# Residual products placed ahead of step 2's, and step 1's pieces as six products of 256 columns instead of three of 512

## The chip, the cores and the metric

The kernel runs on one core of one Trainium2 chip. The metric is device microseconds of one execution, the median of the runs shown; lower is better. Before the change it is 996.77 us (three runs, 996.63 to 997.63).

## The reference

The input x is 8 batches of 3136 rows of 256 numbers in float32. What is computed is the real part of a two-dimensional Fourier transform, and a normalised two-layer network on it:

```python
X = np.fft.fft(x, axis=1)
X = np.fft.fft(X, axis=2)
x = X.real.astype(np.float32)
mu = np.mean(x, axis=-1, keepdims=True)
var = np.mean((x - mu) ** 2, axis=-1, keepdims=True)
xn = (x - mu) / np.sqrt(var + 1e-06) * g_ln
ch = np.maximum(xn @ w_ch1, 0.0) @ w_ch2
return (x + ch).astype(np.float32)
```

w_ch1 is 256 x 1024 and w_ch2 is 1024 x 256.

## The kernel before

**The work.** The transform along the 3136 rows is done in two steps of smaller products. The symmetry of a real transform is used, so that only 1567 rows and two single ones for each batch pass through the rest; the second half comes out of sums and differences at the end. The transform along the 256 columns is folded into the network's first weights, and is done once more for the sum at the end, the *residual*.

- *Step 1* (`step1`, lines 251 to 269): seven pieces for each batch. The input is folded on GpSimd (`fold_zw`, `fold_eo`) and split into a high part (`fold_hi`, ScalarE) and a low part (`fold_lo`, GpSimd), both float32r. Each piece is multiplied by the table t1 in three passes (`PASSES`, line 341: high table with low piece, low table with high piece, high with high), each one product of 512 columns (line 266). All three add up in one bank of PSUM. ScalarE copies it out (line 269), and it goes to device memory and comes back in another order (`store1`, `relayout`). Batch 0 is done in another way ahead of the main loop (lines 259 and 261).
- *Step 2* (`step2`, lines 303 to 339): 64 units, eight for each batch. A unit is four float32 products of 98 or 99 columns (line 313); the first unit of a batch has another of 50 columns (line 317). The profile shows each float32 product as two instructions, so eight records for a unit. The result is a stretch of rows of the transform, and is cut into *chunks* of 256: ScalarE writes the high part (line 334) and a full copy (line 336), VectorE the low part (line 338). A unit can end in two chunks.
- *Network, first layer* (`moe1_a`, line 358): six float32r products of 256 columns for one chunk and one of eight groups of hidden units; ScalarE and VectorE make sum and difference of their two halves (lines 363 to 365). `moe1_b` (lines 372 and 373) applies the maximum with zero and splits the result into high and low parts.
- *Network, second layer* (`moe2`, line 408): twelve float32r products of 256 columns, added up in two banks (tags `acc0` and `acc1`, for even and odd chunks) over the eight groups.
- *Residual* (`residual`, lines 430 to 440): for each chunk two halves (c, 0) and (c, 1), each two float32 products of 129 and 130 columns (line 438), eight records in the profile. `residual_e` (ScalarE) and `residual_y` (VectorE) take it out of PSUM and make mean and variance; `finish` (lines 483 to 490, VectorE) adds the network's result, and `store_out` writes it.

**The order.** All engines but SyncE run in an order that is written out by hand (`tc.manual_schedule`). The main loop (lines 836 to 843) goes through *slots*, eight for each chunk, s = 8c + f:

```python
moe1_b(s - 1)
moe1_a(s)
for fn, args in late.get(s, ()):
    fn(*args)
moe2(s - lag)
for fn, args in after.get(s, ()):
    fn(*args)
```

A slot thus has six products of line 358 and twelve of line 408, all float32r and 256 columns wide, and whatever `late` and `after` hold for it. Everything else is placed in these two lists by lines 616 to 684:

- Step 2's units stand in `after` of slot 8c + 5, for those whose first row falls into chunk c + 1 (lines 626 to 636). Most of these slots have one unit, fourteen have two. The second unit of a slot uses the bank of PSUM with tag `y`, the first that with tag `fft`. The low part (line 338) is made in `late` of the next slot.
- The residual of chunk c stands in `after` of the same slot 8c + 5 (line 666), added after step 2's units. The only exception is chunk 37, where it is inserted ahead of them (lines 670 and 671). I call such a slot, and the eight up to the next of its kind, *block* c. A block with two units is a *double* block. Blocks 0 and 1 have the residual in slots of their own.
- The residual's two banks are those of `acc` that the chunk before has used: (c, 0) needs line 489 of half 0 of chunk c - 1 to be done, (c, 1) that of half 1, which stands in `late` of slot 8c + 4.
- In batches 2 to 7 five of the seven pieces of step 1 stand in the slot behind such a group: one slot later in a block with one unit, two slots later in a double block (`behind`, lines 637 to 639). The other two are at `need - 46` and `need - 45 - b % 2` (line 645), so that in batches 3, 5 and 7 two pieces share a slot. Step 1 uses the bank with tag `y`; of two pieces in one slot the second uses `fft` (`joined`, lines 247 to 249).
- A piece's loads, folds and casts are placed at fixed distances ahead of its slot, its store behind it (lines 653 to 663).

**Shapes.** The residual's first product has 129 columns, its second 130. A table (`shape`, lines 426 to 428) gives, for 12 blocks (7, 13, 19, 25, 31, 40 and 42 to 47), another width (130) to the first product or another order of the two, for one half or both.

Of the kernel before, what the change touches and what calls it, by code (L numbers as in the profile page):

```python
# [20 lines left out]
F32 = mybir.dt.float32  # L21
# [13 lines left out]
LC = NCH - 1  # L35
# [111 lines left out]
def tile_kernel(ctx: ExitStack, tc: tile.TileContext, x, g_ln, w1, w2, tu, tab, tz, ty, tw, out):  # L147
    nc = tc.nc
# [4 lines left out]
    psum = ctx.enter_context(tc.tile_pool(name="psum", bufs=1, space=bass.MemoryType.PSUM))  # L153
# [8 lines left out]
    t1_hi = weights.tile([128, 128], F32R, name="t1_hi")  # L162
    t1_lo = weights.tile([128, 128], F32R, name="t1_lo")
# [6 lines left out]
    ty_s = const.tile([128, 2, 130], F32, name="ty_s")  # L170
# [57 lines left out]
    def alloc1(b):  # L228
        if b not in s1:
            s1[b] = work.tile([128, NS, 2, 128], F32, tag="s1", name=f"s1_{b}", bufs=1)  # L230
            scratch[b] = dram.tile([NS, 128, D], F32, tag="scratch", name=f"scratch{b}")
# [12 lines left out]
        if p1 == NS:  # L244
            nc.scalar.copy(zmu[:, b % 2, 127:128], ps[:KP, 2, 0:1])

    def joined(b, i):

        return i > 0 and steps1[b][i] == steps1[b][i - 1]

    def step1(b, i):
        alloc1(b)
        ps = psum.tile([128, 2, 2, 128], F32, name=f"ps1_{b}_{i}", bufs=1 if b else 2,
                       tag=("fft" if joined(b, i) else "y") if b else f"acc{i % 2}")
        if b == 0:
            z, w = zw.pop((b, i))
            for h in range(2):
                o = ps[:, :, h]
                nc.tensor.matmul(o, tu_s[:, 0:128], z, start=(h == 0), stop=False,  # L259
                                 skip_group_check=True)  # L260
                nc.tensor.matmul(o, tu_s[:, 128 * h:128 * h + 128], w, start=False, stop=True,  # L261
                                 skip_group_check=True)
        else:
            p = pieces.pop((b, i))
            for n, (ti, xi) in enumerate(PASSES):
                nc.tensor.matmul(ps, (t1_hi, t1_lo)[ti], p[xi],  # L266
                                 start=(n == 0), stop=(n == 2))
        s = s1[b][:, 2 * i:2 * i + 2]
        nc.scalar.copy(s[:, :, :, :127], ps[:, :, :, :127])  # L269

# [18 lines left out]
    def first_token(m):  # L289
        b, j = divmod(m, 8)  # L290
        return b * REG + max(gb[2 * j] - 2, 0)
# [102 lines left out]
    acc = {}  # L394
# [21 lines left out]
    def mixed():  # L416
# [6 lines left out]
                                op0=ALU.mult)  # L423
        mixes.append(t)

    shape = {(7, 0): (130, 0), (13, 1): (130, 0), (19, 0): (130, 0), (19, 1): (130, 0),
             (25, 0): (129, 1), (25, 1): (129, 1), (31, 1): (129, 1),
             **{(c, 0): (130, 0) for c in (40, 42, 43, 44, 45, 46, 47)}}

    def residual(c, i):  # L430
        ps = psum.tile([128, 2, 130], F32, tag="y" if i > 1 else f"acc{(c + 1) % 2}",
                       name=f"psy{c}_{i}", bufs=1 if i > 1 else 2)
        t0 = 120 if i == 3 else 128 * i
        ck = mixes.pop() if i == 2 else chunk[c][0][:, :, t0:t0 + 128]
        n0, j0 = shape.get((c, i), (129, 0))
        for j in (j0, 1 - j0):
            n = (n0, 130)[j]
            nc.tensor.matmul(ps[:, j, :n], ck[:, j], ty_s[:, j, :n], start=(j == j0), stop=True,  # L438
                             skip_group_check=True)
        res[c, i] = ps  # L440

    def residual_e(c, i):
# [160 lines left out]
    def finish_w2(n):  # L603
        _, e, f = conv.pop(f"w2_{n}")
        nc.vector.scalar_tensor_tensor(out=f, in0=f, scalar=2.0 ** -20, in1=e, op0=ALU.mult,
                                       op1=ALU.mult)
        return f
# [8 lines left out]
    after, late = {}, {}  # L616

    def add(s, fn, *args):

        after.setdefault(s, []).append((fn, args))  # L620

    def add_late(s, fn, *args):

        late.setdefault(s, []).append((fn, args))

    first = {}
    for m in range(3, 64):
        s = 8 * (first_token(m) // CW) - 3
# [8 lines left out]
    def behind(s):  # L637

        return s + 1 + (len(first[s]) > 1)

    steps1 = {1: [17, 20, 23, 26, 28, 30, 33]}
    casts = dict(zip(steps1[1], (12, 15, 20, 22, 23, 27, 28)))
    for b in range(2, NB):
        need = 8 * (b * REG // CW) - 3
        steps1[b] = sorted([need - 46, need - 45 - b % 2] +
                           [behind(need - d) for d in (56, 40, 32, 24, 16)])
    for b in range(1, NB):
        need = 8 * (b * REG // CW) - 3
        at = steps1[b]
        ends_at = need - (30 if b == 1 else 57 if b == 2 else 58)  # L650
        add(need - 62 if b > 1 else ends_at - 7, ends, b)
        add(ends_at, step1_ends, b)
        for i, d in enumerate(at):
            d0, d = d, d - (b == 1)
            add(d - 7, fold_zw, b, i, nc.gpsimd)
            if b + 1 < NB:
                add(d - 5, load_x, b + 1, i)
            add(d - 6, fold_eo, b, i)
            cast = casts[d0] if b == 1 else (d - 4, d - 3)[d % 8 == 6]
            add(cast, fold_hi, b, i)  # L660
            add(cast + 1, fold_lo, b, i)
            add(d0, step1, b, i)
            add(d0, store1, b, i)
        add(at[-1] + 2, relayout, b)
    for c in range(LC):
        s = 8 * c + (5 if c > 1 else 6)
        add_late(8 * c + 9 + (c < 2), std, c)
        add_late(8 * c + 10 + (c < 2), inverse_std, c)
        for i in range(2):
            if c == 37:  # L670
                after[s].insert(i, (residual, (c, i)))
            else:
                add(s, residual, c, i)
            add_late(s + 1, residual_e, c, i)
            add_late(s + i + 2, residual_y, c, i)
            add_late(8 * c + 11 + i, finish, c, i)
            add(8 * c + 11 + i, store_out, c, i)
# [3 lines left out]
    for i, (r, e, y) in ((2, (1, 2, 2)), (3, (3, 4, 4)), (0, (4, 5, 5)), (1, (5, 6, 6))):  # L681
        add(8 * LC + r, residual, LC, i)
        add_late(8 * LC + e, residual_e, LC, i)
        add_late(8 * LC + y, residual_y, LC, i)
# [11 lines left out]
    with tc.manual_schedule(engines={E.PE, E.Activation, E.DVE, E.Pool}):  # L696
        with tc.manual_schedule(engines={E.SP}):
# [21 lines left out]
            ends(0, 0, 6)  # L719
            fold_zw(0, 0, nc.vector)  # L720
            step1(0, 0)
            nc.vector.tensor_scalar_mul(g_s, g_s, 2.0 ** -20)
            fold_zw(0, 1, nc.vector)
            convert_z("w1_0", w1p[0])
            step1(0, 1)
            convert_m("w1_0", w1p[0])
            fold_zw(0, 2, nc.vector)
# [61 lines left out]
            f = finish_w2(0)  # L789
# [8 lines left out]
            f = finish_w2(1)  # L798
# [18 lines left out]
            f = finish_w2(2)  # L817
# [51 lines left out]
```

## Time and profile before

| | |
|---|---|
| time, median of three runs | 996.77 us |
| time of the profiled execution | 997.91 us |
| its span, first to last instruction | 996.1 us |
| TensorE clock granted | 0.998 |
| TensorE matmuls | 987.3 us busy (99%), 8288 |
| VectorE, ScalarE, GpSimd | 82%, 54%, 25% |
| products of line 408, three groups of 1568 | 435.0, 434.7 and 434.7 us |
| products of line 358, three groups of 768 | 219.2, 214.1 and 213.6 us |
| products of step 2 (line 313), 512 records | 65.6 us |
| products of step 1 (line 266), 3 x 49 | 57.9 us |

The median and the profiled execution differ by 1.1 us, of which 0.9 us also separate the fastest and the slowest of the three runs. Durations of matmuls in a profile overlap, since they are pipelined and their ends are modelled: 1568 products of 277 ns each don't take 435 us of the span. What elapses is read from starts, or from the chain of waits, whose pieces lie end to end. In lines of instructions the columns are start, duration, engine, source line, operation, what is written and read, shape and count; in the chain they are start, length, engine, what is written, source line and count. PE is TensorE's matmuls, PEld its weight loads, PEldq the sequencer in front of them, DVE VectorE, ACT ScalarE and POOL GpSimd.

### The profile page before, as it was taken

The numbers are of one execution on the slowest core, as the hardware profiler recorded it, in microseconds if no ns is written. First come the engines' busy times: TensorE is split into PE (matmuls) and PEld (weight loads), VectorE is DVE, ScalarE is ACT, GpSimd is POOL, SyncE is SP. The second block draws the span as 40 slices with busy tenths as digits, with TensorE's granted clock in tenths as the row PEclk, the third lists the DMA queues.
The fourth block names the chain that finished last, engine by engine and source line by source line (L and its number), as shares of the span: only waits on it lengthen the run. The fifth ranks groups of instructions, "written<-read, shape, count | busy, mean of one in ns | idle before, by whom it ended". The sixth has DMA issues, their size and how long they took to land.

```text
span 996.1 us, 21760 instructions
## 1 busy us (share of the span) xinstructions
PE 987.3 (99%) x8288; PEld 966.8 (97%) x8289; DVE 812.9 (82%) x2190; ACT 535.7 (54%) x1416; POOL 250.1 (25%) x278
## 2 busy tenths in 40 slices
PE   9999999999999999999999999999999999999998
PEld 6799999999999999999999999999999999999998
DVE  6688887888878788888888888888788878888887
ACT  3556555555555555555555555555555554555553
POOL 2156333113412332322342224113322300000000
PEclk9999999999999999999999999999999999999999
DMA  9943352214221252111521242211310113100101
GB/s 348 257 155 121 105 177 78 86 54 138 86 94 55 75 145 100 60 69 64 170 82 58 85 128 96 91 59 64 118 54 33 54 43 97 37 29 22 44 22 43
DMA packets 41528, 92.10 MB, mean 92 GB/s; under 512 B 4176, under 2 KB 18704, under 8 KB 40528
## 3 DMA queue, kind: packets, MB, share of 16 engines
q1 hardware_dynamic: 40016, 88.87, 27.3%
q8 instruction: 66, 1.08, 0.5%
q0 software_dynamic: 320, 1.05, 0.3%
q10 hardware_dynamic: 1088, 0.79, 0.2%
q14 instruction: 38, 0.31, 0.1%
HBM read 50.32 MB, written 40.37 MB: 91 GB/s over the span
## 4 chain that ended last, share of the span: by engine, by line
PE 93%; DVE 3%; DMA 2%; ACT 1%; issue 0%; SPq 0%; ACTq 0%; DVEq 0%
PE acc L408 51%; PE ab L358 26%; PE ps L313 6%; PE psy L438 4%; PE ps L266 3%; DVE h_lo L373 1%; PE ps L259 1%; PE ps L261 1%; DMA scratch<-s 1%; DVE h L364 1%; DMA s<-scratch 1%; DVE h L365 1%; DMA xs<-x 0%; ACT h_hi L372 0%; ACT asb L363 0%
## 5 line engine op out<-in xcount | busy, mean ns | idle before, releaser
L408 PE MATMUL acc<-w_hi,h_lo 128*128 128x256 f32 x1568 | 435.0, 277 | 0.2 <-DVE h_lo L373 0.2
L408 PE MATMUL acc<-w_lo,h_hi 128*128 128x256 f32 x1568 | 434.7, 277 | 0.0
L408 PE MATMUL acc<-w_hi,h_hi 128*128 128x256 f32 x1568 | 434.7, 277 | 0.0
L373 DVE SCALAR_TENSOR_TENSOR h_lo<-h,h_hi 128x512 fp32r<-128x512 f32 x392 | 291.9, 745 | 149.2 <-ACT h_hi L372 147.0
L372 ACT ACTIVATE h_hi<-h 128x512 fp32r<-128x512 f32 x392 | 250.0, 638 | 294.5 <-DVE h L365 293.8
L408 PEld LDWEIGHTS acc<-w_lo,h_hi 128*128 128x128 f32 x1568 | 295.3, 188 | 0.0
L408 PEld LDWEIGHTS acc<-w_hi,h_hi 128*128 128x128 f32 x1568 | 294.9, 188 | 0.0
L408 PEld LDWEIGHTS acc<-w_hi,h_lo 128*128 128x128 f32 x1568 | 294.3, 188 | 0.6 <-DVE h_lo L373 0.4
L358 PE MATMUL ab<-ckl,w_hi 128*128 128x256 f32 x768 | 219.2, 285 | 1.1 <-DVE h L365 1.1
L358 PE MATMUL ab<-ckh,w_lo 128*128 128x256 f32 x768 | 214.1, 279 | 0.7 <-ACT w_lo L601 0.4
L358 PE MATMUL ab<-ckh,w_hi 128*128 128x256 f32 x768 | 213.6, 278 | 0.0
L225 POOL TENSOR_TENSOR fl<-f,fh 128x512 fp32r<-128x512 f32 x49 | 65.5, 1339 | 511.0 <-ACT fh L219 465.7
L364 DVE TENSOR_TENSOR h<-asb,ab 128x256 f32<-128x256 f32 x384 | 158.8, 414 | 2.3 <-ACT asb L363 2.1
L365 DVE TENSOR_TENSOR h<-asb,ab 128x256 f32<-128x256 f32 x384 | 158.8, 414 | 0.0
L358 PEld LDWEIGHTS ab<-ckl,w_hi 128*128 128x128 f32 x768 | 144.8, 189 | 4.1 <-ACT w_hi L549 0.9
L358 PEld LDWEIGHTS ab<-ckh,w_lo 128*128 128x128 f32 x768 | 145.2, 189 | 3.3 <-ACT w_lo L601 0.6
L358 PEld LDWEIGHTS ab<-ckh,w_hi 128*128 128x128 f32 x768 | 145.1, 189 | 0.0
L363 ACT COPY asb<-ab 128x256 f32<-128x256 f32 x384 | 138.2, 360 | 11.3 <-PE ab L358 8.2
L313 PE MATMUL ps<-tab_s,s 112*128 112x98 f32 (+1 forms) x512 | 65.6, 273 | 1.3 <-DMA s<-scratch 1.3
L269 ACT COPY s<-ps 128x508 f32<-128x508 f32 x56 | 32.8, 585 | 63.1 <-PE ps L266 49.4
L334 ACT CAST ckh<-ps 128x392 fp32r<-128x392 f32 (+49 forms) x112 | 39.7, 355 | 44.9 <-PE ps L313 44.7
L313 PEld LDWEIGHTS ps<-tab_s,s 112*128 112x128 f32 x512 | 61.8, 191 | 1.7 <-issue 1.7
(108 smaller groups left out, 963.3 us busy)
## 6 DMA issues: line engine op xcount, KB each, us to landing
xs<-x SPq DMA_DIRECT2D x56, 512.0 KB, 4.5
out<-o SPq DMA_DIRECT2D x96, 256.0 KB, 2.0
scratch<-s SPq DMA_DIRECT2D x49, 256.0 KB, 2.3
s<-scratch SPq DMA_DIRECT2D x7, 1792.0 KB, 9.7
w1p_all<-w SPq DMA_DIRECT2D x8, 512.0 KB, 8.7
scratch<-s POOLq DMA_DIRECT2D x4, 256.0 KB, 6.4
s<-scratch SPq DMA_DIRECT2D x2, 448.0 KB, 5.7
s<-scratch SPq DMA_DIRECT2D x1, 896.0 KB, 11.9
```

The lines of the kernel that those rows point to most:

```text
L225: nc.gpsimd.tensor_tensor(out=lo, in0=f, in1=hi.bitcast(F32), op=ALU.subtract)
L269: nc.scalar.copy(s[:, :, :, :127], ps[:, :, :, :127])
L313: nc.tensor.matmul(ps[:, h, k0 - base:k1 - base], s2[b][:KP, g, 128 * h:128 * h + 128], tab_s[:, h, k0:k1], start=(h == 0 and g == 2 * j), ...
L334: nc.scalar.copy(hi, src)
L358: nc.tensor.matmul(pt, wt[wi][:, j, fs], ch[xi][:, j, :w], start=(n == 0), stop=(n == 2))
L363: nc.scalar.copy(asb[:, :w], pa)
L364: nc.vector.tensor_tensor(out=h[:, :w], in0=asb[:, :w], in1=pb, op=ALU.add)
L365: nc.vector.tensor_tensor(out=h[:, w:], in0=asb[:, :m], in1=pb[:, :m], op=ALU.subtract)
L372: nc.scalar.activation(h_hi, h, AF.Relu)
L373: nc.vector.scalar_tensor_tensor(out=h_lo, in0=h, scalar=0.0, in1=h_hi.bitcast(F32), op0=ALU.max, op1=ALU.subtract)
L408: nc.tensor.matmul(acc[c, i][:, side], hs[xi][:, h0:h0 + 128], ws[wi][:, f], start=(f == 0 and side == 0 and n == 0), stop=(f == 7 and n = ...
L438: nc.tensor.matmul(ps[:, j, :n], ck[:, j], ty_s[:, j, :n], start=(j == j0), stop=True, skip_group_check=True)
```

## The change

- In all blocks from 2 on, but for 5, 11, 17, 23, 29, 35 and 41, the residual's products are inserted ahead of step 2's units in `after` of slot 8c + 5 (39 blocks, of which one, 37, had that already). In the seven blocks left, one of the units is the first of a batch, with the extra product of 50 columns. What ScalarE and VectorE do keeps its place in their order.
- The table of shapes goes: the residual's products are 129 and 130 columns wide in all blocks, in that order.
- Each of step 1's three passes becomes two products of 256 columns, one for each half of the bank: six products in place of three, with the same tables loaded for each.
- The two pieces of batches 3, 5 and 7 that shared a slot get slots of their own: the second, with its folds, casts, load and store, comes one slot later. All pieces use the bank with tag `y`.

```diff
     def step1(b, i):
-        ps = psum.tile([128, 2, 2, 128], F32, name=f"ps1_{b}_{i}", bufs=1 if b else 2,
-                       tag=("fft" if joined(b, i) else "y") if b else f"acc{i % 2}")
+        ps = psum.tile([128, 2, 2, 128], F32, tag="y" if b else f"acc{i % 2}", name=f"ps1_{b}_{i}",
+                       bufs=1 if b else 2)
...
             for n, (ti, xi) in enumerate(PASSES):
-                nc.tensor.matmul(ps, (t1_hi, t1_lo)[ti], p[xi],
-                                 start=(n == 0), stop=(n == 2))
+                for a in range(2):
+                    nc.tensor.matmul(ps[:, a], (t1_hi, t1_lo)[ti], p[xi][:, a],
+                                     start=(n == 0 and a == 0), stop=(n == 2),
+                                     skip_group_check=True)
...
-    shape = {(7, 0): (130, 0), (13, 1): (130, 0), (19, 0): (130, 0), (19, 1): (130, 0),
-             (25, 0): (129, 1), (25, 1): (129, 1), (31, 1): (129, 1),
-             **{(c, 0): (130, 0) for c in (40, 42, 43, 44, 45, 46, 47)}}
...
     def residual(c, i):
-        n0, j0 = shape.get((c, i), (129, 0))
-        for j in (j0, 1 - j0):
-            n = (n0, 130)[j]
-            nc.tensor.matmul(ps[:, j, :n], ck[:, j], ty_s[:, j, :n], start=(j == j0), stop=True,
-                             skip_group_check=True)
+        for j in range(2):
+            nc.tensor.matmul(ps[:, j, :129 + j], ck[:, j], ty_s[:, j, :129 + j],
+                             start=(j == 0), stop=True, skip_group_check=True)
...
-        steps1[b] = sorted([need - 46, need - 45 - b % 2] +
+        steps1[b] = sorted([need - 46, need - 45] +
                            [behind(need - d) for d in (56, 40, 32, 24, 16)])
...
+    def ahead(c):
+
+        return c > 1 and (c % 6 != 5 or c == LC - 1)
+
     for c in range(LC):
         s = 8 * c + (5 if c > 1 else 6)
         for i in range(2):
-            if c == 37:
-                after[s].insert(i, (residual, (c, i)))
-            else:
-                add(s, residual, c, i)
+            after.setdefault(s, [])
+            after[s].insert(i if ahead(c) else len(after[s]), (residual, (c, i)))
```

LC is 48, the number of the last chunk.

More of the change, by code (lines that the diff above doesn't have):

```diff
@@ L245, in step1_ends @@
             nc.scalar.copy(zmu[:, b % 2, 127:128], ps[:KP, 2, 0:1])
-    def joined(b, i):
-        return i > 0 and steps1[b][i] == steps1[b][i - 1]
     def step1(b, i):
         alloc1(b)
-        ps = psum.tile([128, 2, 2, 128], F32, name=f"ps1_{b}_{i}", bufs=1 if b else 2,
-                       tag=("fft" if joined(b, i) else "y") if b else f"acc{i % 2}")
+        ps = psum.tile([128, 2, 2, 128], F32, tag="y" if b else f"acc{i % 2}", name=f"ps1_{b}_{i}",
+                       bufs=1 if b else 2)
         if b == 0:
```

## The prediction

> **What bounds the kernel now.** I read the page first: busy shares, then the shares of the chain that ended last.
>
> ```profile
> PE 987.3 (99%) x8288; PEld 966.8 (97%) x8289; DVE 812.9 (82%) x2190; ACT 535.7 (54%) x1416; POOL 250.1 (25%) x278
> ...
> PE 93%; DVE 3%; DMA 2%; ACT 1%; issue 0%; SPq 0%; ACTq 0%; DVEq 0%
> ```
>
> TensorE is busy for 99% of the span and makes 93% of the chain, so the time is the sum of its products plus its few stops. A change that adds or removes no product can only move the time by the pace at which products follow one another. A product's own duration hides that, because ends are modelled and overlap. The chain of waits shows it: its pieces lie end to end, so their lengths (second column) are elapsed time. Here it is around block 37, the one block whose residual already stands in front of step 2.
>
> ```profile
> 775.13 0.89 PE psy L438 x8
> 776.03 0.87 PE ps L313 x8
> 776.90 0.72 PE ab L358 x6
> 777.62 1.36 PE acc L408 x12
> 778.98 0.69 PE ps L266 x3
> 779.67 0.71 PE ab L358 x6
> 780.38 0.71 PE acc L408 x6
> ```
>
> Now an ordinary block with the residual behind step 2, two blocks later:
>
> ```profile
> 814.38 0.87 PE ps L313 x8
> 815.25 0.92 PE psy L438 x8
> 816.17 0.71 PE ab L358 x6
> 816.88 1.41 PE acc L408 x12
> 818.29 0.70 PE ps L266 x3
> 818.99 0.69 PE ab L358 x6
> ```
>
> The same twelve products take 1.36 us in one place and 1.41 us in the other: 113 or 118 ns each, with nothing waited for. TensorE has two paces, and each lasts until something that isn't a 256-column product comes along. Residual last leaves the slow pace, whichever came in. Residual first (block 37) leaves the fast one. A piece of step 1 as three products of 512 flips the pace: after block 37's (778.98) six L408 products take 0.71, the slow pace; after the other (818.29) L358 takes 0.69, fast but for its start.
>
> To see how much of the run is slow I counted the chain's pieces from 64 us to 963 us. First and last of the 88 L408 pieces at 1.41, first and last of the 279 at 1.36, first of the 219 L358 pieces at 0.68 (87 are at 0.71, the last of them the 816.17 above), and the first of step 1's 43 single pieces (17 at 0.69, 26 at 0.70; the other six come as three pairs):
>
> ```profile
> 65.00 1.41 PE acc L408 x12
> ...
> 70.12 1.36 PE acc L408 x12
> ...
> 960.82 1.36 PE acc L408 x12
> ...
> 77.14 0.68 PE ab L358 x6
> ...
> 79.18 0.69 PE ps L266 x3
> ```
>
> The last at 1.41 is the 816.88 above. A quarter of the run goes at the slow pace. None of it stands directly behind the seven ordinary-looking blocks that the change leaves alone (5, 11, 17, 23, 29, 35, 41): with their 50 extra columns they already end fast.
>
> **The change, part by part.** Products: the same 129 and 130 columns, the same 98; the table of shapes removes a column or two in 12 blocks. I sum against the profiled execution (997.91 us, span 996.1), which lies 1.1 us above the median of 996.77; the difference found is then taken from the median.
>
> *Slow pace removed.* If the moved blocks end like block 37 and six products of 256 columns keep the pace they find, the slow stretches go. L408: 88 x 0.05 = 4.4 us. L358: 26 of the 87 stand directly behind an unshaped residual; there 0.92 + 0.71 becomes 0.89 + 0.72, 26 x 0.02 = 0.5 us; the other 61 go from 0.71 to 0.68, 1.8 us. In the 12 blocks with a shape
>
> ```profile
> 871.52 0.92 PE psy L438 x8
> 872.44 0.70 PE ab L358 x6
> 873.13 1.36 PE acc L408 x12
> ```
>
> the pace is fast already, and 0.92 + 0.70 becomes 0.89 + 0.72: 0.1 us in all. Together 6.8 us.
>
> That twelve blocks have two step 2's (16 L313 products, not 8) should not matter: residual last leaves the same slow pace behind 8 and behind 16.
>
> *Step 1.* Six products of 256 columns look like L358's and L408's, the same operands from the same pools, so I price them at 0.68 (the L358 row) against 0.695: 49 x 0.015 = 0.7 us saved. Each brings its own weight load, 147 more in all. The page has one load for each product (8289 and 8288), they overlap, and 0.68 has a load in each of its six, so that is in the price. Bounds: 0.68 and, were a product of 256 to run at the slow pace, 0.71, 0.7 us lost. TensorE: Matmul & The Clock Gate (the Trainium skill, Back-to-back issue gap) speaks against this part: it gives N/2.4 + 2.5 ns, an estimate of 655 ns for six against 647 for three, so 0.4 us more over 49; no row here shows either, the trace has 113 ns where the page has 109.
>
> Pieces (3,2), (5,2) and (7,2), which stood in one slot with their neighbour, come one slot later, with their folds on POOL, their input load and their store on SP's queue. They use bank y after their neighbour, as batches 2, 4 and 6 do already without a stop. I cost that at nothing; its cover is that slot of 2 us, and without it each would cost the copy between them, some 0.6 us.
>
> *The wait that comes in.* With residual last, ScalarE and VectorE empty step 2's banks while TensorE does the residual. With residual first that cover of 0.89 us is gone. The last L338 (the low half of the chunk), against the first product behind the group: an ordinary single block, block 37, and a double block with the L266 load that comes next on bank y.
>
> ```profile
> 562.47 0.36 PE L358 MATMUL ab<-ckl,w_hi 128*128 128x256 f32 x1
> 564.66 0.63 DVE L338 TENSOR_TENSOR ckl<-ps,ckh 128x234 fp32r<-128x234 f32 x2
> ...
> 776.68 0.37 PE L358 MATMUL ab<-ckl,w_hi 128*128 128x256 f32 x1
> 779.76 0.62 DVE L338 TENSOR_TENSOR ckl<-ps,ckh 128x382 fp32r<-128x382 f32 x2
> ...
> 543.16 0.36 PE L358 MATMUL ab<-ckl,w_hi 128*128 128x256 f32 x1
> 546.01 0.44 DVE L338 TENSOR_TENSOR ckl<-ps,ckh 128x278 fp32r<-128x278 f32 x1
> 547.24 0.19 PEld L266 LDWEIGHTS ps<-fl,t_hi 128*128 128x128 f32 x1
> ```
>
> Single: L338 ends 564.66 + 0.63 - 562.47 = 2.82 us behind the group. Block 37: 779.76 + 0.62 - 776.68 = 3.70. So it comes 0.88 later. In a single block nobody waits: step 1 there uses bank y and step 2 the other. In a double block the second step 2 has bank y, and step 1, two slots later, needs it back. L338 ends 3.29 behind the group, the load starts at 4.08: 0.79 spare. With 0.88 less the load stands 0.09 short, and the wait itself goes through TensorE's sequencer:
>
> ```profile
> L266 PEldq EVENT_SEMAPHORE  x47: 51/51/51, 77.0 to 816.0; - x47
> ```
>
> It takes 51 ns; with as much again to see the semaphore and to start, an estimate from that row, 0.1 to 0.15 us. I take 0.23 us for each of the eleven moved double blocks with a step 1 behind them: 2.5 us. Queued behind it on TensorE is everything, so it is lost in full. Bounds: nothing (if the copies catch up) and 0.5 each, 5.5 in all. Below nothing is excluded: no queue gets shorter.
>
> *Pace after that wait.* A stop restarts the stream, at either pace. Two waits of the trace:
>
> ```profile
> 64.06 0.94 PE ab L358 x6
> ...
> 84.11 0.84 PE ab L358 x6
> 84.96 1.36 PE acc L408 x12
> ```
>
> The first (0.94, against 0.68) leaves 1.41 at 65.00, the second (0.84) leaves 1.36. One each way; I take four in ten slow. Six slots of 0.05 + 0.03 remain to the next residual, 0.48 us: 11 x 0.48 x 0.4 = 2.1 us, bounds 0 and 5.3.
>
> *Residual's bank.* Residual (c,1) needs the bank that the preceding block's last finish frees (L489, out of acc). In block 37 it ends at 774.70 + 0.47 = 775.17, 0.04 behind the chain's 775.13, without a wait; in block 2 at 89.53, 0.40 behind the group's 89.13:
>
> ```profile
> 774.70 0.47 DVE L489 SCALAR_TENSOR_TENSOR o<-acc,r,y 128x256 f32<-128x256 f32 x1
> ...
> 89.06 0.47 DVE L489 SCALAR_TENSOR_TENSOR o<-acc,r,y 128x256 f32<-128x256 f32 x1
> ...
> 89.13 1.76 PE ps L313 x16
> ```
>
> That is 0.36 later than a time that cost nothing; the four products of residual (c,0) cover part. 0.2 us, once; bounds 0 and 0.36. Later blocks lie near block 37.
>
> Sum: -6.8 - 0.7 + 2.5 + 2.1 + 0.2 = -2.7: 995.2 in a profiled execution, **994.1** as a median.
>
> **The rivals.** *The wait stays hidden.* Then the 2.5 and the 2.1 fall away: 996.8 - 7.5 + 0.2 = 989.5. For it: the margin is missed by tenths only. Against it: block 37 has the delay in full, and the spare 0.79 is smaller.
>
> *The slow pace stays (slower).* Three products of 512 flip a slow pace to fast. Six that flip nothing also rescue nothing. If step 2 last leaves the slow pace, a moved block stays slow through all eight slots: 8 x 0.08 = 0.64 us, 39 blocks 25 us, less the 6.8 that are slow now: 996.8 - 0.7 + 18 = 1014. It turns the sign from about 15 blocks on (7.5 + 2 us over 0.64). Against it stands block 37. For it: block 37 is one block, and step 2 without a residual, last in its group, once left the slow pace (45.73: the ten L408 products from 47.34 to 48.40 come every 1.06/9 = 118 ns):
>
> ```profile
> 45.73 1.03 PE L313 MATMUL ps<-tab_s,s 112*128 112x98 f32 x8
> ...
> 47.34 0.28 PE L408 MATMUL acc<-w_hi,h_lo 128*128 128x256 f32 x1
> ...
> 48.40 0.28 PE L408 MATMUL acc<-w_hi,h_lo 128*128 128x256 f32 x1
> ```
>
> and once the fast one (the 1.36 at 70.12 stands behind such a group). It would have to depend on the block, through buffers or through the pace before it.
>
> *Only the double blocks end slow.* Sixteen products leave another phase than eight. Twelve blocks are slow for two slots (1.9 us), the wait shrinks by that 0.1 each (1.4 us stay), and every one stays slow behind step 1 (5.3): 996.8 - 7.5 + 0.2 + 1.9 + 1.4 + 5.3 = 998.1, within 0.2% of now.
>
> **How the numbers follow.** My forecast (wait comes, mixed paces after it) gets 0.57; with none or all of the eleven slow behind it, it goes from 992.0 to 997.3. Wait hidden 0.18; slow pace stays 0.15; only the doubles slow 0.10. The range from 988.9 to 998.3 takes in the first two and the last, and leaves out the 0.15 of the slow pace and a little at the edges. About 0.2% (2 us) is what a measurement of this kernel can tell from no change. Faster: 0.18, and 0.44 of the 0.57 (those with up to about half slow), with a little for doubles: 0.63. Same: 0.12 and 0.07: 0.19. Slower: 0.15 and 0.03: 0.18.
>
> **What would show it.** Right: in the chain, psy 0.89 before ps 0.87 in 39 blocks, then 1.36 as good as everywhere; step 1's six products at 0.68 with the pace before them kept; in eleven double blocks a piece of VectorE's L338 or idle time in front of L266, some 0.2 us. Wrong: rows of 1.41 behind the moved blocks without a wait before them, or behind step 1; step 1 above 0.70; no idle time in front of L266 in block 38; or a time under 989 or over 998.

## The result, and the profile after

The changed kernel takes 998.35 us (median of 20 runs, 996.39 to 1000.38), the kernel before 996.84 us beside it (20 runs, 995.79 to 999.78). The ratio is 1.0015, 95% interval 1.0008 to 1.0022: slower by 0.15%, or 1.5 us, where the prediction had 994.1 us and faster as the likeliest. The interval leaves out a ratio of 1, but the step is less than the 2 us below which the prediction counted a time as the same. The profiled execution of after took 998.37 us, span 996.6 us; before, 997.91 and 996.1.

The page of after, as before: engines, then the chain that ended last.

```profile
PE 988.1 (99%) x8436; PEld 970.4 (97%) x8436; DVE 811.5 (81%) x2190; ACT 529.3 (53%) x1416; POOL 247.8 (25%) x278
...
PE 91%; DVE 5%; ACT 2%; DMA 1%; issue 1%; ACTq 0%; SPq 0%; DVEq 0%
```

There are 148 records of matmuls more, 147 of them step 1's. TensorE's share of the chain went from 93% to 91%, VectorE's from 3% to 5%: TensorE now waits somewhere.

What was meant to happen did. The chain of waits around block 37:

```profile
775.08 0.72 PE ab L356 x6
775.80 1.36 PE acc L406 x12
777.16 0.68 PE ps L263 x6
777.84 0.68 PE ab L356 x6
```

Step 1 now takes 0.68 as six products, and the fast pace goes on behind it (before, 0.71 followed). All moved groups in this trace end fast like this, with one unit or two, and whichever pace they came in with, but for two of those with a wait in the group itself (blocks 43 and 47, below; 2, 45 and 46 have one too and end fast).

Two other things came with it. First, the double blocks. Two of them in the chain, and the wait of the first one in the lines of instructions:

```profile
213.38 0.93 PE ps L263 x6
214.31 0.71 PE ab L356 x6
215.01 1.41 PE acc L406 x12
...
291.78 0.92 PE ps L263 x6
...
293.38 1.36 PE acc L406 x12
```

```profile
212.12 1.10 DVE L336 TENSOR_TENSOR ckl<-ps,ckh 128x392 fp32r<-128x392 f32 x3
...
213.33 0.30 PEld L263 LDWEIGHTS ps<-fl,t_hi 128*128 128x128 f32 x2
```

VectorE's low part ends at 213.22, step 1's first weight load starts 0.11 us later, and the six products take 0.93 in place of 0.68. Behind it the stream goes on at 118 ns (1.41); behind the second one, whose wait looks the same, at 113 ns (1.36). All eleven have the wait; eight of the eleven are slow behind it.

Second, the late blocks. Block 43 in the chain, and its finish:

```profile
886.54 0.45 PE psy L430 x4
886.99 0.02 issue
887.01 0.71 PE psy L430 x4
```

```profile
886.38 1.34 PE L430 MATMUL psy<-ty_s,ck 128*128 128x129 f32 x8
886.48 0.47 DVE L481 SCALAR_TENSOR_TENSOR o<-acc,r,y 128x256 f32<-128x256 f32 x1
...
887.00 0.52 PEld L430 LDWEIGHTS psy<-ty_s,ck 128*128 128x128 f32 x4 [0.21 <-DVE o L481]
```

The group starts at 886.38, the finish that frees the bank of residual (c,1) ends at 886.95, 0.57 us later, and the second half's first load waits for it. In the kernel before, the finish of this block is 0.30 us ahead of its group (887.84 + 0.47 against 888.61):

```profile
887.84 0.47 DVE L489 SCALAR_TENSOR_TENSOR o<-acc,r,y 128x256 f32<-128x256 f32 x1
...
888.61 1.03 PE L313 MATMUL ps<-tab_s,s 112*128 112x98 f32 x8
```

The same wait is in blocks 45, 46 and 47. In the trace of before, block 37, whose finish the prediction read (774.70 + 0.47 = 775.17), has its group's first product at 774.97, so there the finish ends 0.20 us behind the group's start. (The prediction's 0.04 is the same margin against the chain, whose piece starts at 775.13; by the chain, block 43 of after has 0.41.)

```profile
774.97 1.05 PE L438 MATMUL psy<-ty_s,ck 128*128 128x129 f32 x8
```

Last, in chunk 48, whose first layer needs more than one bank, the product behind `aa` starts 0.80 us after it (before: 0.28). The waits of after name VectorE for it (the columns are the sum of the waits, their number and the longest):

```profile
PEld bb L356 <- DVE h L363: 1.0, 2, 0.7
```

**Where the time went.** The two traces were laid over each other by the first L356 (L358) product of each slot. After less before is -1.6 us at 80 us of the span, -2.2 at 880 and +0.4 at 973, and stays there to the end. The start varies: it is -0.2 to -1.6 us in the kernels below, and the profiled execution of before was itself 1.1 us above its median. Between 80 and 880 us the change gained 0.6 us, and between 880 and 973 it lost 2.7.

### The profile page after: what moved, and what is told of

Its sections match the earlier page's. It is cut to its first block, busy times and chain, and to the rows that moved or that the text cites. A ratio compares the mean times of both kernels' runs of the same rounds, so it can differ in the third digit from the quotient of the medians.

```text
span 996.6 us, 22061 instructions
## 1 busy us (share of the span) xinstructions
PE 988.1 (99%) x8436; PEld 970.4 (97%) x8436; DVE 811.5 (81%) x2190; ACT 529.3 (53%) x1416; POOL 247.8 (25%) x278
## 4 chain that ended last, share of the span: by engine, by line
PE 91%; DVE 5%; ACT 2%; DMA 1%; issue 1%; ACTq 0%; SPq 0%; DVEq 0%
PE acc L406 50%; PE ab L356 25%; PE ps L311 5%; PE psy L430 4%; PE ps L263 4%; DVE h_lo L371 2%; DVE h L362 1%; DVE h L363 1%; ACT h_hi L370 1%; PE pw L687 1%; PE ps L255 1%; PE ps L257 1%; DMA scratch<-s 1%; DMA s<-scratch 0%; DVE st L452 0%
## 5 line engine op out<-in xcount | busy, mean ns | idle before, releaser
L406 PE MATMUL acc<-w_hi,h_lo 128*128 128x256 f32 x1568 | 434.4, 277 | 0.1
L406 PE MATMUL acc<-w_lo,h_hi 128*128 128x256 f32 x1568 | 434.2, 277 | 0.0
L406 PE MATMUL acc<-w_hi,h_hi 128*128 128x256 f32 x1568 | 434.2, 277 | 0.0
L370 ACT ACTIVATE h_hi<-h 128x512 fp32r<-128x512 f32 x392 | 250.1, 638 | 297.3 <-DVE h L363 297.1
L406 PEld LDWEIGHTS acc<-w_hi,h_lo 128*128 128x128 f32 x1568 | 294.9, 188 | 0.4 <-DVE h_lo L371 0.3
L406 PEld LDWEIGHTS acc<-w_lo,h_hi 128*128 128x128 f32 x1568 | 294.7, 188 | 0.0
L406 PEld LDWEIGHTS acc<-w_hi,h_hi 128*128 128x128 f32 x1568 | 294.5, 188 | 0.0
L356 PE MATMUL ab<-ckl,w_hi 128*128 128x256 f32 x768 | 218.7, 285 | 1.8 <-DVE h L363 1.7
L356 PE MATMUL ab<-ckh,w_lo 128*128 128x256 f32 x768 | 213.2, 278 | 0.5 <-ACT ckh L332 0.3
L356 PE MATMUL ab<-ckh,w_hi 128*128 128x256 f32 x768 | 212.8, 277 | 0.0
L356 PEld LDWEIGHTS ab<-ckl,w_hi 128*128 128x128 f32 x768 | 144.6, 188 | 3.3 <-ACT w_hi L541 1.4
L356 PEld LDWEIGHTS ab<-ckh,w_lo 128*128 128x128 f32 x768 | 144.5, 188 | 0.9 <-ACT ckh L332 0.5
L356 PEld LDWEIGHTS ab<-ckh,w_hi 128*128 128x128 f32 x768 | 144.2, 188 | 0.0
```

Source lines behind the costliest of these rows:

```text
L356: nc.tensor.matmul(pt, wt[wi][:, j, fs], ch[xi][:, j, :w], start=(n == 0), stop=(n == 2))
L370: nc.scalar.activation(h_hi, h, AF.Relu)
L406: nc.tensor.matmul(acc[c, i][:, side], hs[xi][:, h0:h0 + 128], ws[wi][:, f], start=(f == 0 and side == 0 and n == 0), stop=(f == 7 and n = ...
```

## The experiments

Theory: the moved order and the six products together take the slow pace away (some 7.5 us), and two waits give it back, those of the double blocks with a slow pace behind most of them, and those of the late blocks. Rivals: the six products themselves cost time; or the order of the residual brings no gain at all, only the pace does.

Slow products are counted below as L356/L406 products (by their lines in each kernel) from 67 us on that stand directly behind another of them and start 116 to 119.5 ns after it; each costs some 4.4 ns against the fast pace. The times are medians, the ratios those to runs of before taken beside each kernel (their medians lie between 996.84 and 997.35), the spans those of the profiled execution.

| kernel | us, median | ratio to before, 95% | span | slow products |
|---|---|---|---|---|
| before | 996.84 | | 996.1 | 1613 |
| after | 998.35 | 1.0015 (1.0008 to 1.0022) | 996.6 | 1183 |
| order_alone | 1011.40 | 1.0139 (1.0122 to 1.0156) | 1009.7 | 3962 |
| six_alone | 1002.83 | 1.0055 (1.0041 to 1.0068) | 1000.8 | 2950 |
| banks_swapped | 993.27 | 0.9958 (0.9946 to 0.9970) | 991.5 | 850 |
| tail_behind | 997.31 | 1.0002 (0.9991 to 1.0013) | 994.1 | 1182 |
| swapped_tail | 989.44 | 0.9923 (0.9910 to 0.9937) | 987.5 | 247 |
| behind_wide | 989.33 | 0.9920 (0.9907 to 0.9932) | 987.6 | 273 |
| full_later | 994.53 | 0.9974 (0.9963 to 0.9985) | 991.7 | 515 |
| swapped_full | 993.20 | 0.9954 (0.9942 to 0.9967) | 991.7 | 651 |
| swapped_filled | 997.44 | 1.0001 (0.9992 to 1.0011) | 995.6 | 325 |

**order_alone**: after, with step 1's three products of 512 columns.

```diff
-                for a in range(2):
-                    nc.tensor.matmul(ps[:, a], (t1_hi, t1_lo)[ti], p[xi][:, a],
-                                     start=(n == 0 and a == 0), stop=(n == 2),
-                                     skip_group_check=True)
+                nc.tensor.matmul(ps, (t1_hi, t1_lo)[ti], p[xi],
+                                 start=(n == 0), stop=(n == 2))
```

> The changed kernel with step 1's pieces put back to three products of 512 columns; the residual stays in front. Theory A (paces and waits): the groups end at the fast pace, 1.36 us for twelve products, but a piece of three 512s flips it to the slow one. In the 21 single blocks from 2 to 39 that leaves seven slots of 0.05 + 0.03 us slow, 21 x 0.56 = 11.8 us; in the eleven double blocks the wait comes as in the changed kernel and the pace behind it is a toss. About 10 us above the changed kernel's 998.35, so 1007 to 1010. Theory B (the six products and their 147 additional loads are what costs): faster than the changed kernel, at or below before's 996.8.

1011.4 us, 1.4 above the range expected; 2779 slow products more than after has make 12.2 of the 13.1 us between the two. A moved block in its chain:

```profile
784.27 0.90 PE psy L428 x8
...
786.76 1.36 PE acc L404 x12
788.12 0.69 PE ps L262 x3
788.81 0.71 PE ab L354 x6
789.52 1.41 PE acc L404 x12
```

The block leaves its group fast, three products of 512 turn it slow, and nothing turns it back for the seven slots to the next group. (Not every moved group turns it back: those at 310 and 956 us came in slow and left slow.) The six products are the part that lets the order gain anything; that they cost time falls.

**six_alone**: before, with step 1's six products alone.

> The kernel before with nothing changed but step 1's pieces as six products of 256 columns. Theory A: six products keep the pace they find, and a residual behind step 2 leaves the slow one, so the 26 unshaped blocks are slow through all eight slots: 26 x 0.64 = 16.6 us less the 6.8 us that are slow before, less 0.7 for step 1: about 1006. In the chain, rows of 1.41 go on behind step 1. Theory B: 49 pieces cost a little more each, 997 to 999, and the pace behind step 1 is as before.

1002.8 us: the direction is right, the size smaller. Two groups of its chain:

```profile
797.29 1.41 PE acc L410 x12
798.70 1.76 PE ps L315 x16
800.46 0.92 PE psy L440 x8
...
802.09 1.41 PE acc L410 x12
...
817.64 1.41 PE acc L410 x12
819.05 0.87 PE ps L315 x8
819.92 0.92 PE psy L440 x8
...
821.54 1.36 PE acc L410 x12
```

Both come in slow and have the residual last. The first leaves slow, the second fast. Eighteen blocks of this kernel run slow from end to end (141 products each), often every other one. One of them is block 37, where the residual stands in front: it came in slow, had no wait in its group and left slow. So a residual of 129 and 130 columns in last place doesn't fix the pace, and one in front doesn't either; what does, the runs leave open.

**banks_swapped**: after, with the two banks of a double block exchanged. The first unit gets `y`, the second `fft`, so that step 1 needs the bank that is emptied first.

```diff
-            second.add(m)
+            second.add(first[s][0])
```

> The changed kernel with the two banks of a double block's step 2 units exchanged: the first unit has the bank that step 1 needs next, the second the other one, so that bank is free about 0.55 us earlier. Theory A: the waits in front of step 1 in the eleven double blocks go (2.6 us in the changed kernel's profile), and so do the slow stretches behind eight of them (8 x 0.48 = 3.9 us): 998.35 - 6.5 = 992. Rival C (the order itself costs, since ScalarE and VectorE are late after every moved residual): the wait moves on to another product, and the time stays within 1 us of 998.

993.3 us, where 992 was expected. The same double block as above:

```profile
213.43 0.68 PE ps L263 x6
214.11 0.68 PE ab L356 x6
214.79 1.36 PE acc L406 x12
```

No wait here or in the ten others, and the fast pace behind all but block 2, which was slow before it. The medians differ by 5.1 us from after, the two traces by 5.7 at 880 us, ahead of the late waits: that is the price of the double blocks. Laid over the trace of before like after, this kernel stands at -8.0 at 880 us and at -4.7 at 973: the late blocks still take 3.3: waits of residual (c,1) in blocks 43 and 45 (0.28 each), a stop of 0.2 at 913 us, chunk 48's wait (0.79), and three blocks slow from end to end, 43, 45 and 46 (424 products, 1.9 us); 46 has no wait of its own and takes the slow pace over from 45.

**tail_behind**: after, with the residual behind step 2 again from block 40 on, with 130 columns in its first product.

```diff
-            nc.tensor.matmul(ps[:, j, :129 + j], ck[:, j], ty_s[:, j, :129 + j],
+            n = 130 if i == 0 and c >= 40 and c != 41 and c < LC else 129 + j
+            nc.tensor.matmul(ps[:, j, :n], ck[:, j], ty_s[:, j, :n],
...
-        return c > 1 and (c % 6 != 5 or c == LC - 1)
+        return 1 < c < 40 and c % 6 != 5
```

> The changed kernel, but with the residual behind step 2 from block 40 on, and there with 130 columns in the first product of half 0, as before. Theory A: from block 42 on no step 1 gives VectorE time to catch up, and residual (c, 1) waits for the last finish: 0.28, 0.07, 0.27 and 0.27 us in blocks 43, 45, 46 and 47, the slow pace through block 43 (0.64) and about 0.9 between the last group and the last chunk. All of that goes: 998.35 - 2.3 = 996. The waits in the double blocks stay. Rival C: the end of the run is bound by ScalarE and VectorE whatever the order is, and the time stays at 998.

997.3 us as a median, 995.9 in the profiled execution, where 996 was expected. By the medians alone the gain against after is not shown, since the two intervals overlap; the traces show it, and so does the step from banks_swapped to swapped_tail below. The finish of block 43 ends 885.83 + 0.48 = 886.31, ahead of its group, at 886.76 in the chain, and the block goes through without a stop:

```profile
885.83 0.48 DVE L482 SCALAR_TENSOR_TENSOR o<-acc,r,y 128x256 f32<-128x256 f32 x1
```

```profile
886.76 0.87 PE ps L311 x8
887.63 0.92 PE psy L431 x8
...
889.25 1.36 PE acc L406 x12
```

All the late waits are gone, and the one in chunk 48 is back at 0.28. In exchange blocks 39 and 40 are slow throughout, 283 products or 1.2 us. Block 39 is a moved one without a wait: it came in slow, from behind the wait of block 38, and its group left it slow; block 40, with the residual behind and 130 columns, then stayed slow too. Two other moved groups of this trace came in slow from behind a wait (those of 543 and 661 us) and left fast. In its eleven double blocks seven are slow behind the wait, not the same ones as in after: those at 213, 349 and 409 us in after are fast here, those at 467 and 799 slow. The code there is the same in both, so what sets the pace behind the wait changes from one execution to another.

**swapped_tail**: both edits together.

> The changed kernel with the banks of a double block's units exchanged and the residual behind step 2 from block 40 on (130 columns in the first product of half 0 there). Theory A: neither the waits in front of step 1 nor those of the last blocks are left. The profile with the banks exchanged still had 0.7 us of waits for the last finish, some 0.7 at the last chunk and 2.0 us of slow pace behind blocks 43 to 47; without them 993.3 - 3.4 = 990, up to 991.5 if a block or two near 40 stays slow as in the profile with the last blocks changed alone. Rival C (ScalarE and VectorE bind the end of the run): 993.

989.4 us, 989.23 to 990.50 in five runs. Against before this trace stands at -8.65 at 880 us and at -8.64 at 973: the late loss is nothing. Against banks_swapped (992.17 to 993.79), from which it differs in the last blocks alone, it gains 3.8 us, and no run of one lies in the range of the other. Against after, the two edits gain 5.1 and 1.0 us as medians when each stands alone, and 8.9 together. Of the 2.8 us more, 1.2 are blocks 39 and 40 of tail_behind, which took over the slow pace from behind a wait that this kernel doesn't have, and 0.6 the larger late loss of banks_swapped (3.3 against 2.7); the rest the runs leave open.

**behind_wide**: step 1's six products and its slots as in after, but the residual behind step 2 in every block, with 130 columns in its first product in those that the change had moved.

```diff
-            n = 129 + j
+            n = 130 if i == 0 and 1 < c < LC and (c % 6 != 5 or c == LC - 1) else 129 + j
...
-        return c > 1 and (c % 6 != 5 or c == LC - 1)
+        return False
```

> Six products for step 1's pieces, the residual behind step 2 in all blocks, and 130 columns in the first product of half 0 in each block that the change would have moved. Theory A: it is the pace that the order buys, and a column more buys the same without giving up the cover; blocks with that shape left the fast pace before (12 of them), so nearly nothing is slow and nothing waits: 996.8 - 6.8 - 0.7 = 989.3, each block that ends slow adding 0.64. Rival D (the order itself shortens something): above the kernel with exchanged banks, 994 or more.

989.3 us. One block of it:

```profile
805.89 0.87 PE ps L311 x8
806.76 0.92 PE psy L431 x8
...
808.38 1.36 PE acc L406 x12
809.74 0.68 PE ps L263 x6
```

No order was changed at all, and the gain is the same as with the order and both waits mended. The residual's place in front is worth only the pace that it leaves, and one more column buys that as well, without a wait. This version beats both kernels, by 0.8% the one before.

**full_later**: after, with ScalarE's full copies of step 2 (L334) taken out of the group and put into the next slot, behind the high part and the maximum (L370). In after they stand ahead of the maximum.

```diff
-            add(s, step2, m, "mhf")
+            add(s, step2, m, "mh")
+        for m in ms:
+            add_late(s + 1, step2, m, "f")
```

> The changed kernel with step 2's full copies on ScalarE behind the next slot's sum copy, in front of the residual's, and not ahead of the maximum. Theory A: what makes the low parts and the last finish late is that the copies stand on ScalarE ahead of the maximum (L370) and come 0.9 us later; with half of them out of the way the low part of a double block comes some 0.5 us earlier, which is more than the 0.23 us that were missing, and VectorE has less to catch up in the last blocks: 998.35 - 6.5 = 992, or 1 us less where the last waits shrink too. Rival C (the order itself makes the engines late): 997 to 999.

994.5 us, 2.5 above what was expected. The finish of block 43 in this trace:

```profile
883.09 0.47 DVE L481 SCALAR_TENSOR_TENSOR o<-acc,r,y 128x256 f32<-128x256 f32 x1
...
883.32 1.05 PE L430 MATMUL psy<-ty_s,ck 128*128 128x129 f32 x8
```

It ends at 883.56, 0.24 us behind the group's start instead of 0.57, and the residual's eight products run through. In the double blocks the wait is left in two of eleven. So ScalarE's copies ahead of the maximum do carry a large part of both delays. Two late waits of some 0.2 us stay (blocks 42 and 45), and the 0.79 of chunk 48 too; the late loss is 0.8 us (from -5.3 to -4.5) instead of 2.7. Some of the gain is lost near the start: this trace stands at +0.5 us against before at 122 us, where after stands at -1.3. It has a stop of 0.5 us at 101 us and 205 slow products more than after between 67 and 125 us (0.9 us). swapped_tail, without this edit, has a stop of 0.4 us in the same slot, so that the edit causes it is not shown.

**swapped_full**: banks_swapped and full_later together.

> Both: banks of the double blocks exchanged and the full copies later, the residual in front in all 39 blocks. Theory A: no wait in front of step 1, and shorter or no waits for the last finish: 990 to 992. Rival C: as with the banks exchanged alone, 993.

993.2 us, no better than banks_swapped alone: the late loss is 1.4 us instead of 3.3, but this trace is 1.3 us behind banks_swapped at 122 us, with a stop of 0.8 us in the slot in which full_later has its own, and 2.2 behind at 160, since blocks 3 and 4 came in slow and left slow (moved ones, without a wait). A late block is slow throughout as well (142 products from 920 us on). A miss: later copies shorten the late waits and don't take them away.

**swapped_filled**: banks_swapped, with six products of 256 columns more in six of the late blocks, to see whether it is the time that step 1 takes on TensorE that protects the earlier ones. Nobody uses their result.

```diff
+    for c in (40, 42, 43, 44, 45, 46):
+        add(8 * c + 6, fill, c)
```

> The kernel with the two banks of double blocks exchanged (993.3 us), with six products of 256 columns more, in the slot behind the group of blocks 40 and 42 to 46, into bank y; their result is used by nobody. No block from 40 on has a piece of step 1, and these products take its time on TensorE (0.68 us each, 4.1 us in all). Theory: in the late blocks VectorE and ScalarE have no spare time against TensorE in which to make up for the copies that the moved residual puts later; up to block 39 the 0.7 us of a piece of step 1 gives it. Then the last finish ends at about +0.2 us behind the start of the group in blocks 41 to 47 instead of up to +0.56, the waits of residual (c,1) (0.28, 0.1 and 0.28 us) and the slow stretches of some 140 products behind two of them go (1.3 us), and the wait in the last chunk gets shorter than 0.79 us: some 995.0 us, 1.7 above and not 4.1. Rival, the residual in front makes the finish late whatever TensorE has to do: the waits stay, and the time is 993.3 + 4.1 = 997.4 us.

997.4 us, which is the rival's number, but for another reason. Block 43 in the lines of instructions and in the chain, then block 44:

```profile
881.46 0.48 DVE L490 SCALAR_TENSOR_TENSOR o<-acc,r,y 128x256 f32<-128x256 f32 x1
...
882.00 1.05 PE L439 MATMUL psy<-ty_s,ck 128*128 128x129 f32 x8
```

```profile
882.16 0.89 PE psy L439 x8
...
884.64 1.36 PE acc L415 x12
886.00 0.68 PE fill L306 x6
...
906.57 0.60 DVE ckl L345 x2
907.17 0.02 issue
907.19 0.83 PE fill L306 x5
```

The finish ends at 881.94, 0.06 us ahead of the group, where banks_swapped without the filling has it at 0.56 behind; no residual waits from block 41 on, and no late block is slow throughout. In block 44, a double block, the filling was put into the slot directly behind the group, needed bank `y` before VectorE had emptied it, and stopped TensorE for 1.66 us: a fault of this experiment. The trace accounts for the rest. Against before it goes from -7.9 at 806 us (ahead of the first filling) to -2.2 at 954; the 5.7 us are six fillings of 0.68 and this stop. Without the stop that is 995.8 us, against 995.0 by the theory, and the rival would have 997.4 + 1.7 = 999.1. The waits show the theory right in block 43; from block 45 on the stop in block 44 gave ScalarE and VectorE time as well. Its last point was not: chunk 48 still waits, 0.93 us.

## Why the prediction was wrong, step by step

The sign was wrong, and the value off by 4.3 us; 998.35 lies at the range's upper edge, just outside it.

- *Slow pace removed* and *step 1*, -7.5 together: right. swapped_tail, in which neither wait is left, gains 7.1 us between 80 and 880 us and 7.8 as a median against its own runs of before. Moved groups with one unit or two end fast in after, so the rivals "the slow pace stays" and "only the double blocks end slow" are out for after. The first of them, as "the pace before it", holds at times where a moved group comes in slow: block 39 of tail_behind, block 46 of banks_swapped, blocks 3 and 4 of swapped_full and block 37 of six_alone stayed slow without a wait. In after all seven moved groups that came in slow left fast; no run shows why, so that part of the term's fit is luck. Six products take 0.68 and keep whichever pace they find (0.71 in tail_behind's slow block 39). The trace has 0.68 for six against 0.69 or 0.70 for three. The estimate of 0.4 us more over 49 went by the formula of the Trainium skill (TensorE: Matmul & The Clock Gate, Back-to-back issue gap), which that section gives for an isolated product; the trace does not agree, the measurement decides, and the part didn't cost that.
- The reason given for it was too strong. "Residual last leaves the slow pace, whichever came in" is false as a rule: six_alone has both outcomes. The sum didn't rest on it, since all moved blocks of after but 43 and 47, which have a wait, ended fast.
- *The wait in the double blocks*, +2.5: right. Eleven came, nine of 0.25 us (0.93 less 0.68) and two of 0.3: 2.8.
- *Pace after that wait*, +2.1, four in ten slow: too small, and here the step was a choice from two waits of one trace. Eight of eleven were slow in one execution, seven of eleven in another. Some 750 slow products of 4.4 ns are 3.3 us; two of the eight stretches ended early. With the wait the double blocks took some 6.5 us between 80 and 880 us (-0.6 in after against -7.1 in swapped_tail) where the prediction had 4.6; some 0.4 of that is in neither count.
- *Residual's bank*, "Later blocks lie near block 37": this is the step that failed, 2.7 us where the sum had nothing. (The 0.2 us that it had for block 2 came.) Block 37 has a piece of step 1 in its block, and so 0.7 us more of TensorE's time in which ScalarE and VectorE make up for what the moved order puts later. From block 40 on there is none. The lag then carries over from one block to the next, and the finish ends 0.57 us behind the group's start in block 43 instead of 0.20 in block 37. What it is made of: waits of 0.28, 0.07, 0.27 and 0.27 us in blocks 43 and 45 to 47; block 43 slow from end to end behind its wait, 140 products, 0.6 us; 85 slow products more, 0.4; chunk 48's wait, 0.5 longer. That is 2.4 of the 2.7; 0.2 of the rest is a stop at 918 us, in block 44. tail_behind and swapped_tail take it away by the order; swapped_filled takes the waits for the finish away by giving TensorE as much to do as block 37 has; full_later shows that ScalarE's copies carry part of it.

In sum -7.1 + 6.5 + 2.7 = +2.1 us, less the 1.6 of the start: the 0.5 us between the two profiled executions. The medians are 1.5 us apart, since the execution of before that was profiled lay 1.1 above its median. The prediction had looked at all banks in block 37, the one block that had the new order, and had taken its margin for that of the rest; the rows of block 43 were in the trace of before, with nothing of step 1 behind them.

The chances had the right shape in one respect: a forecast whose gain of 7.5 us is taken back by waits was the likeliest, and the wait of the double blocks was named. What decided the sign were two terms of 1.2 and 2.7 us, in a sum of -2.7.

## What to carry to other kernels

A margin read from one instance of a block holds for blocks with the same work on every engine; where one kind of work ends before the loop does, read the last blocks on their own. When a product stream has two paces, look for the cheapest thing that leaves it in the fast one (here a column more) before moving work: an order that moves the copies behind it later pays for the pace with waits. And a stop costs more than its length if the stream may restart at the slower pace.

## What the runs showed of the hardware

- A stream of float32r products of 256 columns, each with its weight load, runs at 113.3 or at 117.7 ns for each (means over the traces of before and after), and holds either for a hundred products and more. It isn't the clock: the profile of before gives a granted clock of 1.00 both for 312 to 326 us, at the slow pace, and for 331 to 345 us, at the fast one. Six products of the same kind keep it; three of 512 columns, a group of step 2 and residual, or a stop can change it. Which way a group turns it hangs on more than its order and widths: 130 columns in the first product leave it fast in all of behind_wide, block 2 among them, which came in slow, and leave it slow in block 40 of tail_behind, which came in slow too.
- A stop of some 0.25 us restarts the stream at either pace: 15 of 22 slow in two executions (after and tail_behind), and the same place in the code came out both ways.
- One column more in one product of the group before (130 in place of 129) leaves nearly the whole run at the fast pace: 273 slow products in behind_wide. six_alone has 2950, with six products for step 1 too and the residual behind step 2 in all blocks but 37, but with 130 columns or another order in only 12 of them.
